# A feed-forward layer with squared ReLU: every contraction cut into 64-row halves, two matmuls at a time on the row groups of the array

## The chip, the cores and the metric

One NeuronCore of a Trainium2 chip runs the whole program. The metric is the device time of one execution in microseconds (us). "Fast" runs are those that agree with the quickest of their kernel.

The engines by their short names: PE is the matmul engine and PEld its weight loads; ACT, DVE and POOL are the scalar, vector and general-purpose engines; SP only issues transfers here. On the page of the kernel before, a product is a weight load (PEld, 128x128, 98 ns on average) and a matmul of 512 or 288 columns with those weights (PE), whose result goes to `ps`, the tensor that the kernel declares in PSUM as eight banks of 512 columns. "Contraction" is the index that a product sums over.

## The reference

```
B, S, D, F = 1, 2048, 576, 4608          # all bf16
h   = x @ w1 + b1                        # [2048, 4608], contraction over 576
r   = max(h, 0)
out = (r * r) @ w2 + b2                  # [2048, 576],  contraction over 4608
```

The number to keep in mind is 576 = 4.5 x 128. The kernel before gives the array 128 contraction rows at a time (128*128 on its page), so the first product does not fill a whole number of tiles. The second product does: 4608 = 36 x 128.

## The kernel before

x is used transposed, in four blocks of 512 rows of x (`b`). The first product makes 36 tiles of h per block (`f`), each 128 features x 512 rows, in one PSUM bank. Its contraction runs over five tiles of 128; the fifth holds the last 128 features of x, of which the first 64 were already used, and these are set to zero. ACT adds the bias and applies ReLU, DVE squares into `h2T`. The second product of a block is interleaved with the first product of the next block: five matmuls of 512 columns, then eight of 288.

```python
# first product: NJ = 5 tiles, the last one half zeros
for j in range(NJ):
    ins = pe.matmul(ps[:, bank, :], w1_sb[:, j, fs], xT_sb[:, j, bsl(b)],
                    start=(j == 0), stop=(j == NJ - 1))
...
# second product: two column halves of 288, whole 128-row tiles
for h in halves:
    ins = pe.matmul(ps[:, 4 + 2 * (q % 2) + h, 0:DH],
                    h2T[:, b % 2, f, st * P : (st + 1) * P],
                    w2_sb[:, f, h * DH : (h + 1) * DH],
                    start=(f == 0), stop=(f == NF - 1))
...
# DVE: what makes half of the fifth tile zero, and the eviction
dve.memset(xT_sb[0:DTAIL, KT, bsl(b)], 0.0)
...
dve.tensor_tensor(o_sb[...], ps[:, 4 + 2 * (q % 2) + h, 0:DH], b2_sb[...], AluOpType.add)
```

## Time and profile before

| | before |
|---|---|
| time, median of the runs of the first round | 307.97 us (307.55 to 308.4) |
| PE busy | 300.4 of 305.7 us |
| chain that ended last | 98% on PE |
| DVE, ACT busy | 114.5 us, 101.9 us |
| first matmul of the first product, last matmul of the second (starts) | 6.00 us, 302.80 us |

The page of the kernel before, first its engine sums, then its chain of waits, then its costliest groups. A group's columns are: line, engine, operation, output and inputs, shapes, count, busy time in us, mean duration of one in ns, and the engine's idle time just before them with what ended it.

```profile
PE 300.4 (98%) x1887; PEld 187.9 (61%) x1918; DVE 114.5 (37%) x184; ACT 101.9 (33%) x148; POOL 0.7 (0%) x6
...
PE 98%; issue 1%; DVE 0%; POOL 0%; POOLq 0%
...
L255 PE MATMUL ps<-xT_sb,w_sb 128*128 128x512 bf16 x689 | 167.2, 379 | 1.6
L280 PE MATMUL ps<-w_sb,h2T 128*128 128x288 bf16 x1152 | 158.8, 286 | 0.0
L339 DVE TENSOR_TENSOR h2T<-r_sb 128x512 bf16<-128x512 f32 x144 | 99.7, 692 | 152.0 <-ACT r_sb L311 151.9
L359 DVE TENSOR_TENSOR o_sb<-ps,b_sb 128x288 bf16<-128x288 f32 x32 | 13.2, 450 | 31.2 <-PE ps L280 31.2
```

PE never waits for the second product (0.0). 31 of the 720 first-product records are missing from the trace. DVE waits 151.9 us for ACT, which waits for PE. So PE bounds the kernel.

The mean durations 379 and 286 ns are not what a matmul costs, since the next one starts before the record of the last one ends (216 and 122.5 ns from start to start, as shown below). The cost is the distance between two starts, called a slot from here on. The timeline of before in an interleaved stretch (start, length, engine, line, what, count) shows it.

```profile
149.49 0.69 ACT L311 ACTIVATE r_sb<-ps,b_col 128x512 f32<-128x512 f32 x1 [1.37 <-PE ps L255]
...
150.27 1.24 PE L255 MATMUL ps<-xT_sb,w_sb 128*128 128x512 bf16 x5
151.35 1.14 PE L280 MATMUL ps<-w_sb,h2T 128*128 128x288 bf16 x8
151.55 0.69 ACT L311 ACTIVATE r_sb<-ps,b_col 128x512 f32<-128x512 f32 x1 [1.37 <-PE ps L255]
...
152.33 1.24 PE L255 MATMUL ps<-xT_sb,w_sb 128*128 128x512 bf16 x5
```

Five wide matmuls take from 150.27 to 151.35, that is 216 ns each; eight narrow ones take from 151.35 to 152.33, that is 122.5 ns each. The whole program is then 720 x 0.2157 + 1152 x 0.1225 = 155.3 + 141.1 = 296.4 us of matmul slots, which with 6.0 us ahead and 2.9 us after the last start makes the span to within 0.4 us. A gain must remove slots.

### The profile page before, as it was taken

Reading aid. Unit: us, or ns where it says so; the run is one execution under the profiler, and the core shown is the slowest. Engines: PE = TensorE matmul, PEld = TensorE weight load, DVE = VectorE, ACT = ScalarE, POOL = GpSimd, SP = SyncE. Lnnn points to the kernel's source line nnn. Section 1 sums busy time; section 2 is a strip of 40 time slices with the busy share of each in tenths; the row PEclk is TensorE's granted clock in tenths of the full one; section 3 lists DMA queues with packets and bytes.
Section 4 is the critical chain, followed back from the end, with each engine's and each line's share of the span. In section 5 each row is a group of like instructions: output and inputs, shape, how many; then the busy total and the mean of one; then the engine's idle time right before and its main releaser. Section 6 shows DMA issues by size and latency. Waiting matters only on the chain.

```text
span 305.7 us, 4424 instructions
## 1 busy us (share of the span) xinstructions
PE 300.4 (98%) x1887; PEld 187.9 (61%) x1918; DVE 114.5 (37%) x184; ACT 101.9 (33%) x148; POOL 0.7 (0%) x6
## 2 busy tenths in 40 slices
PE   8999999999999999999999999999999999999996
PEld 7444446666666666666666666666666666687874
DVE  2666663343433434334333343433333343311111
ACT  3666663233323323333332333333233333300000
POOL 0000000000000000000000000000000000000000
PEclk9999999999999999999999999999999999999999
DMA  7984996200000000000000000000000000000000
GB/s 222 354 277 91 362 349 119 57 20 0 2 19 0 21 0 20 1 0 21 0 20 2 0 21 0 19 2 0 19 2 19 2 19 0 2 19 23 19 21 19
DMA packets 22579, 16.56 MB, mean 54 GB/s; under 512 B 9376, under 2 KB 22560, under 8 KB 22560
## 3 DMA queue, kind: packets, MB, share of 16 engines
q1 hardware_dynamic: 22224, 15.98, 17.1%
q8 instruction: 15, 0.25, 0.3%
q10 hardware_dynamic: 336, 0.30, 0.3%
q14 instruction: 4, 0.03, 0.0%
HBM read 11.95 MB, written 2.36 MB: 47 GB/s over the span
## 4 chain that ended last, share of the span: by engine, by line
PE 98%; issue 1%; DVE 0%; POOL 0%; POOLq 0%
PE ps L255 50%; PE ps L280 46%; PE ps L207 1%; PE ps L217 1%; DVE o_sb L359 0%; PE ps L227 0%; PE ps L265 0%; POOL ones L197 0%; POOLq L378 0%
## 5 line engine op out<-in xcount | busy, mean ns | idle before, releaser
L255 PE MATMUL ps<-xT_sb,w_sb 128*128 128x512 bf16 x689 | 167.2, 379 | 1.6
L280 PE MATMUL ps<-w_sb,h2T 128*128 128x288 bf16 x1152 | 158.8, 286 | 0.0
L339 DVE TENSOR_TENSOR h2T<-r_sb 128x512 bf16<-128x512 f32 x144 | 99.7, 692 | 152.0 <-ACT r_sb L311 151.9
L311 ACT ACTIVATE r_sb<-ps,b_col 128x512 f32<-128x512 f32 x144 | 98.9, 687 | 161.8 <-PE ps L255 160.7
L280 PEld LDWEIGHTS ps<-w_sb,h2T 128*128 128x128 bf16 x1152 | 112.7, 98 | 48.6
L255 PEld LDWEIGHTS ps<-xT_sb,w_sb 128*128 128x128 bf16 x720 | 70.5, 98 | 64.9 <-ACT xT_sb L133 0.3
L359 DVE TENSOR_TENSOR o_sb<-ps,b_sb 128x288 bf16<-128x288 f32 x32 | 13.2, 450 | 31.2 <-PE ps L280 31.2
L207 PE MATMUL ps<-ones 128*128 128x128 bf16 x22 | 2.5, 313 | 1.1 <-POOL ones L197 1.1
L207 PEld LDWEIGHTS ps<-ones 128*128 128x128 bf16 x22 | 2.3, 147 | 1.0 <-POOL ones L197 1.0
L134 DVE CAST xT_sb<-ps 128x512 bf16<-128x512 f32 x2 | 1.3, 686 | 4.0 <-PE ps L217 4.0
L217 PE MATMUL ps<-ident,x_nat 128*128 128x128 bf16 x20 | 2.3, 309 | 0.0
L217 PEld LDWEIGHTS ps<-ident,x_nat 128*128 128x128 bf16 x20 | 2.1, 143 | 0.3 <-issue 0.3
L133 ACT ACTIVATE xT_sb<-ps 128x512 bf16<-128x512 f32 (+1 forms) x3 | 1.7, 594 | 1.4 <-PE ps L217 1.4
L133 ACT ACT_TABLE_LOAD x1 | 1.3, 1283 | 2.4 <-issue 2.4
L327 DVE MEMSET xT_sb<- 64x256 uint32 x3 | 0.8, 272 | 0.0
L323 DVE COPY b_col<-ps 128x36 f32<-128x36 f32 x1 | 0.2, 195 | 1.0 <-PE ps L265 1.0
L227 PE MATMUL ps<-ones 128*128 128x128 bf16 x3 | 0.5, 311 | 0.0
L317 DVE MEMSET b_nat<- 128x64 uint32 x1 | 0.1, 112 | 0.9 <-PEq L378 0.9
L227 PEld LDWEIGHTS ps<-ones 128*128 128x128 bf16 x3 | 0.4, 147 | 0.0
L199 POOL TENSOR_SCALAR_AFFINE_SELECT ident<-ones 128x128 bf16<-128x128 bf16 x1 | 0.3, 292 | 0.1
L318 DVE MEMSET xT_sb<- 64x256 uint32 x1 | 0.3, 272 | 0.0
L265 PE MATMUL ps<-ident,b_nat 128*128 128x128 bf16 x1 | 0.2, 219 | 0.1
(6 smaller groups left out, 0.7 us busy)
## 6 DMA issues: line engine op xcount, KB each, us to landing
w_sb<-in_w_dram SPq DMA_DIRECT2D x9, 576.0 KB, 8.2
w_sb<-in_w_dram SPq DMA_DIRECT2D x8, 512.0 KB, 6.4
out_dram<-o_sb SPq DMA_DIRECT2D x15, 144.0 KB, 1.7
w_sb<-in_w_dram SPq DMA_DIRECT2D x9, 128.0 KB, 7.3
w_sb<-in_w_dram SPq DMA_DIRECT2D x1, 384.0 KB, 3.6
x_nat<-in_x_dram ACTq DMA_DIRECT2D x2, 144.0 KB, 3.1
x_nat<-in_x_dram SPq DMA_DIRECT2D x2, 144.0 KB, 2.8
b_sb<-in_b_dram SPq DMA_DIRECT2D x1, 144.0 KB, 8.1
```

What stands on the lines that cost most here:

```text
L133: return eng.activation(dst, src, COPY)
L134: return eng.tensor_copy(dst, src)
L199: pool.affine_select(ident[:], ones[:], [[1, P]], AluOpType.is_equal, 0.0, base=0, channel_multiplier=-1).then_inc(s_id, 1)
L207: pe.matmul(ps[:, 0, 0:P], ones[:], ones[:], start=True, stop=True)
L217: ins = pe.matmul(ps[:, TB0 + j, t * P : (t + 1) * P], x_nat[:, t, d0 : d0 + P], ident[:], start=True, stop=True,)
L227: pe.matmul(ps[:, 0, 0:P], ones[:], ones[:], start=True, stop=True)
L255: ins = pe.matmul(ps[:, bank, :], w1_sb[:, j, fs], xT_sb[:, j, bsl(b)], start=(j == 0), stop=(j == NJ - 1),)
L280: ins = pe.matmul(ps[:, 4 + 2 * (q % 2) + h, 0:DH], h2T[:, b % 2, f, st * P : (st + 1) * P], w2_sb[:, f, h * DH : (h + 1) * DH], start=(f ...
L311: act.activation(r_sb[:, g % NR, :], ps[:, g % MM1_BANKS, :], RELU, bias=b1_col[:, f : f + 1]).then_inc(s_act, 1)
L327: dve.memset(xT_sb[0:DTAIL, KT, bsl(b)], 0.0).then_inc(s_xprep, 1)
L339: dve.tensor_tensor(h2T[:, b % 2, f, :], r_sb[:, g % NR, :], r_sb[:, g % NR, :], AluOpType.mult).then_inc(s_sq, 1)
L359: dve.tensor_tensor(o_sb[:, i, h * DH : (h + 1) * DH], ps[:, 4 + 2 * (q % 2) + h, 0:DH], b2_sb[:, h * DH : (h + 1) * DH], AluOpType.add,). ...
```

## The change

Half of every fifth tile multiplies zeros. The change cuts both contractions into 64-row halves. Rows 0 to 63 and rows 64 to 127 of the array (the two row groups) are then to work as two arrays of 64 rows, each with its own weights, its own moving data and its own PSUM bank. In the first product the lower rows make a tile of h from the first half of F and the upper rows one from the second half. 576 is 9 x 64, so nine slots make two tiles of h, where ten were needed before. To let both row groups go through all nine chunks, x is kept in nine tiles that hold each chunk once in the lower and once in the upper partitions; four of these are put together by DVE copies. w1 is laid out in two halves of the partitions. The second product, which has no ragged edge, is halved as well: its two halves land in two banks, and DVE adds them.

```diff
+    LO = [0, 2, 4, 6, 1, 3, 5, 7, 8]      # chunk in the lower rows, by slot
+    HI = [1, 3, 5, 7, 2, 4, 6, 8, 0]      # chunk in the upper rows
 ...
-                    for j in range(NJ):
-                        ins = pe.matmul(ps[:, bank, :], w1_sb[:, j, fs], xT_sb[:, j, bsl(b)], ...)
+                    for h in range(2):
+                        ch_ = LO[j] if h == 0 else HI[j]
+                        ins = pe.matmul(
+                            ps[:, banks[h], :],
+                            w1_sb[HP * h : HP * (h + 1), ch_, cs],
+                            xT_sb[HP * h : HP * (h + 1), j, bsl(b)], ...)
 ...
-                    for h in halves:
-                        ins = pe.matmul(ps[:, 4 + 2 * (q % 2) + h, 0:DH], h2T[:, b % 2, f, ...], w2_sb[:, f, ...], ...)
+                    for h in range(2):
+                        ins = pe.matmul(
+                            ps[:, 4 + 2 * ch + h, 0:DH],
+                            h2T[HP * h : HP * (h + 1), b % 2, f, st * P : (st + 1) * P],
+                            w2_sb[HP * h : HP * (h + 1), f, ch * DH : (ch + 1) * DH], ...)
 ...
-            dve.memset(xT_sb[0:DTAIL, KT, bsl(0)], 0.0).then_inc(s_xprep, 1)
+                dve.tensor_copy(xT_sb[0:HP, j, cs0], xT_sb[HP:P, src_lo, cs0])
+                dve.tensor_copy(xT_sb[HP:P, j, cs0], xT_sb[0:HP, src_hi, cs0]).then_inc(s_asm, 1)
 ...
-                        dve.tensor_tensor(o_sb[...], ps[:, 4 + 2 * (q % 2) + h, 0:DH], b2_sb[...], AluOpType.add)
+                    dve.tensor_tensor(t_sb[:, ch, :], ps[:, 4 + 2 * ch, 0:DH], b2_sb[:, cs], AluOpType.add)
+                    dve.tensor_tensor(o_sb[:, i, cs], ps[:, 5 + 2 * ch, 0:DH], t_sb[:, ch, :], AluOpType.add)
```

(Cut: the interleaving is by slot now, w1 is loaded in 16 transfers of 64 partitions each, and semaphores follow.)

## The prediction

> **What bounds the kernel now.** TensorE. The page's first part has PE busy 300.4 of 305.7 us, and the chain that ended last lies 98% on PE (50% first product, 46% second), with 1.6 us of idle time before all first-product matmuls and none before the second's. The granted clock is full. In the timeline ACT fires every 2.06 us in the interleaved stretches, for 5 matmuls of 512 columns and 8 of 288: 216 and 122.5 ns start to start; the durations shown (379, 286 ns) are latencies. Sum: 720 x 0.2157 + 1152 x 0.1225 = 155.3 + 141.1 = 296.4 us, plus 6.0 us before the first product and 2.5 us after the last matmul: the span. DVE (37%) and ACT (33%) wait for PE.
>
> **What the change removes.** The contraction of the first product is 576 = 4.5 x 128 and is paid as 5 tiles; half the fifth multiplies zeros. As 9 chunks of 64 rows, two on the array at a time (lower rows: one weight column block into one bank; upper rows: another into another bank), it costs 9 slots for two blocks, where it was 10: 648 slots of 512 columns for 720. Gain: 72 x 0.2157 = 15.5 us, all on the critical path. The second product is also halved in rows, 2304 half matmuls in 1152 pairs, with no column saved[...].
>
> **What it adds.**
> - Matmuls and weight loads double (1872 to 3600). A pair of second-product halves must get two weight loads into 122.5 ns. [...]
> - DVE: two additions where one 450 ns addition was (32 more: about 14 us), and 32 copies of 64x512 bf16 within SBUF [...]. DVE goes from 114 to about 137 us of 290: still half idle. Two 687 ns activations free a pair's banks, under the 1.94 us of a pair: no stall.
> - Start: nine x tiles instead of five must be ready in the first pair, four of them by DVE copies of evicted tiles; w1 comes in 64-row pieces with short rows. About +0.5 to 1 us. The end has one more addition: +0.5 us.
>
> **Predicted: 294 us** (307.97 - 15.5 + 1.5), 291 to 304 for 8 times in 10. Chances: faster by over 2% 0.80, within 2% 0.07, slower 0.13.
>
> **What would show it.** Right: starts of the two halves of a pair within tens of ns, pairs at 216 and 122.5 ns; the first product's stretch (ends at 45 us now) some 3.5 us shorter; interleaved stretches with 10% fewer 512-column slots; the closing second-product stretch (34.8 us) unchanged; PE idle under 3 us; DVE near 137 us busy.
>
> **What would make it wrong.** (1) Weight loads or issue limit the short pairs: closing stretch longer than 34.8 us, pairs above 123 ns, say 160 ns; this alone could cost 10 to 45 us and is the main risk. (2) The two row halves don't stream together: 560 us. [...] (4) The start waits for w1, or the second product for w2: gaps before the first matmuls or around 49 us, laid to DMA.

Where a cut is marked, a passage is taken out that no trace showed: why the second product is split, an estimate of two weight loads in series and the conclusion drawn from it, what was said of loads and starts on two row groups, a risk of 7 us that rested on that, and the duration put for one copy. The 1.5 us for start and end is the author's estimate. DVE's 137 us were 114.5 us and 14 us for the additions, and the rest, some 8 us, was for the 32 copies.

## The result

| | before | after |
|---|---|---|
| median | 307.77 us (16 runs, 307.28 to 308.4) | 294.14 us (8 runs, 293.58 to 294.68) |
| ratio | | 0.9554, 95% interval 0.9542 to 0.9565 |
| profiled span | 305.7 us | 292.2 us |
| DVE busy | 114.5 us | 132.9 us |

A ratio is the mean time of one kernel's fast runs over that of the other's of the same rounds, so it is not quite the ratio of the medians quoted. Run again unedited in a later session (after_again), the changed kernel gave 294.06 us (5 runs) and a ratio of 0.955 (0.9534 to 0.9565), as expected:

> The changed kernel itself, unedited, for a comparison in the same rounds with the two versions beside it: 294.1 us, ratio to before 0.955.

The page after, the same parts.

```profile
PE 286.2 (98%) x3646; PEld 181.8 (62%) x3646; DVE 132.9 (45%) x243; ACT 94.6 (32%) x150; POOL 0.7 (0%) x6
...
PE 94%; DVE 3%; DMA 1%; SPq 1%; issue 0%; ACT 0%
...
L333 PE MATMUL ps<-w_sb,h2T 64*128 64x288 bf16 x2304 | 214.6, 283 | 0.0
L306 PE MATMUL ps<-xT_sb,w_sb 64*128 64x512 bf16 x1296 | 210.9, 376 | 1.8 <-DMA w_sb<-in_w_dram 1.1
...
L429 DVE TENSOR_TENSOR h2T<-r_sb 128x512 bf16<-128x512 f32 x144 | 94.2, 689 | 113.3 <-ACT r_sb L380 113.0
...
L452 DVE TENSOR_TENSOR t_sb<-ps,b_sb 128x288 f32<-128x288 f32 x32 | 14.6, 456 | 36.6 <-PE ps L333 36.5
L457 DVE TENSOR_TENSOR o_sb<-ps,t_sb 128x288 bf16<-128x288 f32 x32 | 14.6, 457 | 1.1
L438 DVE COPY xT_sb<-xT_sb 64x512 bf16<-64x512 bf16 x24 | 6.9, 289 | 0.7
```

PE is still the bound. It issues nearly twice the matmuls, and each lasts as long as before (376 and 283 ns), yet the kernel is shorter: two run at a time. PE's busy column for a group has become useless as a cost, because pairs of the two products overlap within it (214.6 + 210.9 us is far more than the span). The timeline of the changed kernel in an interleaved stretch shows the pairs.

```profile
150.02 0.38 PE L306 MATMUL ps<-xT_sb,w_sb 64*128 64x512 bf16 x2
150.24 0.29 PE L333 MATMUL ps<-w_sb,h2T 64*128 64x288 bf16 x2
150.36 0.38 PE L306 MATMUL ps<-xT_sb,w_sb 64*128 64x512 bf16 x2
150.57 0.41 PE L333 MATMUL ps<-w_sb,h2T 64*128 64x288 bf16 x4
150.82 0.38 PE L306 MATMUL ps<-xT_sb,w_sb 64*128 64x512 bf16 x2
```

Two wide matmuls fit into 0.38 us, the length of one, and the next pair starts 0.21 to 0.22 us later. The records themselves, start in us and distance to the previous record of the same engine in ns:

```
150.019 PE          64x512        150.235 PE   +213   64x288        150.357 PE   +119   64x512
150.022 PE     +3   64x512        150.238 PE     +3   64x288        150.360 PE     +3   64x512
150.020 load                      150.236 load +212                 150.359 load +119
150.024 load   +4                 150.240 load   +4                 150.362 load   +3
```

A pair starts within 3 ns here, its two weight loads within 4 ns, and pairs follow each other at 216 and 122 ns: the slots of before. (In the first stretch, where the first product runs alone, the two starts of a pair lie 19 ns apart until 44 us; pairs still follow at 216 ns.)

Where the 13.44 us of the span went, from the starts of the first and last matmuls of the two products:

| stretch | before | after | difference |
|---|---|---|---|
| start of the program to first matmul | 6.00 | 6.82 | +0.82 |
| first to last matmul (start to start) | 296.80 | 282.01 | -14.79 |
| last matmul to the end | 2.86 | 3.39 | +0.53 |

The middle row is 72 slots x 0.2157 = 15.53 us less, and 0.74 us more of stalls. The three small losses, 2.1 us, are the difference between the gain by slots and the gain in the span. This is one profile of each kernel; in after_again the first matmul starts at 6.64 us, so the 0.82 varies by some 0.2 us.

### The profile page after: what moved, and what is told of

Its sections match the earlier page's. It is cut to its first block, busy times and chain, and to the rows that moved or that the text cites. A ratio compares the mean times of both kernels' runs of the same rounds, so it can differ in the third digit from the quotient of the medians.

```text
span 292.2 us, 8040 instructions
## 1 busy us (share of the span) xinstructions
PE 286.2 (98%) x3646; PEld 181.8 (62%) x3646; DVE 132.9 (45%) x243; ACT 94.6 (32%) x150; POOL 0.7 (0%) x6
## 4 chain that ended last, share of the span: by engine, by line
PE 94%; DVE 3%; DMA 1%; SPq 1%; issue 0%; ACT 0%
PE ps L333 48%; PE ps L306 46%; DVE h2T L429 2%; DMA w_sb<-in_w_dram 1%; DVE xT_sb L438 1%; SPq L172 0%; SPq L176 0%; ACT r_sb L380 0%; DVE t_sb L452 0%; DVE o_sb L457 0%
## 5 line engine op out<-in xcount | busy, mean ns | idle before, releaser
L333 PE MATMUL ps<-w_sb,h2T 64*128 64x288 bf16 x2304 | 214.6, 283 | 0.0
L306 PE MATMUL ps<-xT_sb,w_sb 64*128 64x512 bf16 x1296 | 210.9, 376 | 1.8 <-DMA w_sb<-in_w_dram 1.1
L333 PEld LDWEIGHTS ps<-w_sb,h2T 64*128 64x128 bf16 x2304 | 112.2, 94 | 64.3
L429 DVE TENSOR_TENSOR h2T<-r_sb 128x512 bf16<-128x512 f32 x144 | 94.2, 689 | 113.3 <-ACT r_sb L380 113.0
L380 ACT ACTIVATE r_sb<-ps,b_col 128x512 f32<-128x512 f32 x144 | 91.0, 683 | 156.7 <-PE ps L306 156.7
L306 PEld LDWEIGHTS ps<-xT_sb,w_sb 64*128 64x128 bf16 x1296 | 65.5, 94 | 41.3 <-DMA w_sb<-in_w_dram 1.2
L452 DVE TENSOR_TENSOR t_sb<-ps,b_sb 128x288 f32<-128x288 f32 x32 | 14.6, 456 | 36.6 <-PE ps L333 36.5
L457 DVE TENSOR_TENSOR o_sb<-ps,t_sb 128x288 bf16<-128x288 f32 x32 | 14.6, 457 | 1.1
L438 DVE COPY xT_sb<-xT_sb 64x512 bf16<-64x512 bf16 x24 | 6.9, 289 | 0.7
L168 ACT ACTIVATE xT_sb<-ps 128x512 bf16<-128x512 f32 x4 | 2.1, 603 | 1.2 <-PE ps L258 1.2
L401 DVE COPY xT_sb<-xT_sb 64x512 bf16<-64x512 bf16 x4 | 1.2, 290 | 0.2
L402 DVE COPY xT_sb<-xT_sb 64x512 bf16<-64x512 bf16 x4 | 1.1, 287 | 0.1
```

The lines of the kernel that those rows point to most:

```text
L168: return eng.activation(dst, src, COPY)
L306: ins = pe.matmul(ps[:, banks[h], :], w1_sb[HP * h : HP * (h + 1), ch_, cs], xT_sb[HP * h : HP * (h + 1), j, bsl(b)], start=first, stop=last,)
L333: ins = pe.matmul(ps[:, 4 + 2 * ch + h, 0:DH], h2T[HP * h : HP * (h + 1), b % 2, f, st * P : (st + 1) * P], w2_sb[HP * h : HP * (h + 1), f ...
L380: act.activation(r_sb[:, g % NR, :], ps[:, mm1_bank(b, f), :], RELU, bias=b1_col[:, f : f + 1]).then_inc(s_act, 1)
L401: dve.tensor_copy(xT_sb[0:HP, j, cs0], xT_sb[HP:P, src_lo, cs0])
L429: dve.tensor_tensor(h2T[:, b % 2, f, :], r_sb[:, g % NR, :], r_sb[:, g % NR, :], AluOpType.mult).then_inc(s_sq, 1)
```

## The experiments

Eleven edits and one repetition of the changed kernel were run. All gave correct results. Theory: the gain is the 72 wide slots that were removed, and everything else must only not spoil it. The rivals are named with each run.

### 1. The zeros put back (zero_slot)

```diff
-    SLOTS = [0, 1, 4, 2, 5, 3, 6, 7, 8]
+    SLOTS = [0, 1, 4, 2, 5, 3, 6, 7, 8, 9]      # slot 9: both row groups multiply a tile of zeros
```

> Each first-product pair gets a tenth slot that multiplies 64 rows of zeros on both row groups, so the array streams the 720 slots of before again, everything else as in the changed kernel. Theory (the gain is the 72 slots of 512 columns that were removed): 294.1 + 72 x 0.2157 = 309.7 us, about 0.5% above before (its start and end are a little longer). Rival (the packing itself makes slots cheaper or dearer than 216 ns, or the gain comes from the split second product): well off 309.7 us; near 294 if the zero slots cost little.

Measured in three rounds: 308.84 us, ratio to before 1.003 (1.0014 to 1.0047). The page of this run shows the 144 matmuls on zeros beside the 1296 others:

```profile
L314 PE MATMUL ps<-xT_sb,w_sb 64*128 64x512 bf16 x1296 | 211.6, 376 | 0.9 <-DMA w_sb<-in_w_dram 0.8
L314 PE MATMUL ps<-zx,w_sb 64*128 64x512 bf16 x144 | 27.3, 376 | 0.0
```

With the slots of before the time of before is back: +14.7 us over the changed kernel, where 15.5 were expected. The missing 0.8 us lies in the start and the stalls: in the profiled run the first matmul starts at 6.27 us (6.82 in the changed kernel's profile, a start that varies), and from the first to the last matmul 0.6 us is more than slots, where the changed kernel has 1.2. So the gain is the removed slots; packing by itself made a slot neither cheaper nor dearer (pairs at 216 and 122 ns in the changed kernel, as the whole matmuls before).

### 2. The second product left whole (mm2_whole)

```diff
-                    for h in range(2):
-                        ins = pe.matmul(ps[:, 4 + 2 * ch + h, 0:DH], h2T[HP * h : HP * (h + 1), ...], ...)
+                    ins = pe.matmul(ps[:, 4 + 2 * ch, 0:DH], h2T[:, ...], w2_sb[:, ...], ...)
```

and one addition per eviction instead of two. Everything else, the fine interleaving too, stays.

> First product in 64-row pairs, second product back to whole 128-row matmuls of 288 columns, interleaved as finely as in the changed kernel: some 970 changes between row modes. Theory [...]: each change exposes most of the latency of a matmul, 286 - 122 = about 160 ns (estimate), so 294 + 970 x 0.16 = about 450 us, PE starts after a change 160 ns later than the cadence. Rival ([...] the split was needless): 294 us or half a microsecond less, as the second addition at the end falls away.

Two passages that named a mechanism which no run shows are cut there. The 160 ns are an estimate, the length of a matmul's record less its slot.

389.05 us. The direction is the theory's, the size is not: 95 us, not 155. The timeline of this run:

```profile
150.21 0.42 PE L332 MATMUL ps<-w_sb,h2T 128*128 128x288 bf16 x2
150.56 0.39 PE L306 MATMUL ps<-xT_sb,w_sb 64*128 64x512 bf16 x2
150.88 0.42 PE L332 MATMUL ps<-w_sb,h2T 128*128 128x288 bf16 x2
151.24 0.39 PE L306 MATMUL ps<-xT_sb,w_sb 64*128 64x512 bf16 x2
151.56 0.30 PE L332 MATMUL ps<-w_sb,h2T 128*128 128x288 bf16 x1
```

A pair of the first product is now followed after 0.32 us (150.56 to 150.88) instead of 0.22. Call the use of the array as two halves or as a whole its row mode. Over the run the mean distance is 321.9 ns from a pair (its first start) to a whole matmul, where 215.7 is the slot, and 220.1 ns from a whole matmul to a pair, where 122.5 is the slot: 106 and 98 ns lost per change of row mode. A whole matmul that follows a whole one comes after 128.2 ns on average instead of 122.5. Together that is 450 x 106 + 449 x 98 + 702 x 5.7 ns, about 96 us, which is the whole loss. The trace has 899 changes (my expectation had counted 971), so by the time a change costs (389.05 - 294.14 + 0.5) / 899 = 106 ns, the 0.5 us being the addition that falls away at the end. What happens in the array at a change the trace does not show, only what it costs.

### 3. The same, with fewer changes (mm2_whole_coarse)

```diff
-                want = (len(steps) * done) // nslot
+                want = (len(steps) * done) // nslot if it[5] else 0      # only after a pair's last slot
```

> As mm2_whole, but the second product's matmuls come in one block after each first-product pair: 99 changes of row mode instead of 971. Theory (each change costs about 98 ns whatever surrounds it, from mm2_whole: (389.05 - 294.14 + 0.5) / 971): 294.1 - 0.5 + 9.7 = 303.3 us. Rival (what cost 95 us in mm2_whole was the whole matmuls or their fine mixture, not the changes): far from it, above 320 us or near 294.

304.21 us. With the 106 ns of the right count, 99 changes make 10.5 us and 304.1 us are expected; with the 98 ns 303.3. The cost is per change, not per whole matmul. (Its trace has 311 and 218 ns at the changes: 96 ns each.)

### 4. No interleaving at all (blocks)

mm2_whole again, but the order of the blocks is first product of block 0, first of 1, second of 0, first of 2, second of 1, and so on; the tile copies for blocks 2 and 3 are made while a second product runs.

```diff
-        for n in range(NPAIR):
-            for it in mm1_pair(b, n, SLOTS, True, True):
-                items.append(it)
-                ...                                        # 2.3 second-product steps after each slot
+        items += mm1_block(b) + mm2_block(b - 1)
```

> First product in 64-row pairs, second product whole, and each product of a block of 512 rows run without interleaving: 5 changes of row mode in all. Only one addition per eviction. Theory (changes cost 0.1 us each, the split second product is needed only because of the fine interleaving): 294.1 + 0.5 - 0.5 = 294 us, DVE about 19 us less busy than in the changed kernel. Rival (the interleaving hides something else, as evictions of the first product at one pair per 1.94 us): over 296 us with gaps on PE laid to ACT or DVE.

Three rounds: 294.03 us, ratio 0.9541 (0.9525 to 0.9557), the same as the changed kernel's. Five changes of mode cost the 0.5 us that the single addition at the end gives back. DVE was busy 118.3 us instead of 132.9; I had expected 19 us less and it is 14.6, the 32 additions alone (the copies stay). So the split of the second product is not part of the gain. It is the price of interleaving at the grain of single matmuls, and with PE the only bound the interleaving is not needed either.

### 5. The two halves of a pair moved apart (halves_apart)

```diff
-        return [("mm1", b, n, j, ...) for i, j in enumerate(slots)]          # lower, upper, lower, upper ...
+        return [("mm1", b, n, j, ..., h) for h in range(2) for i, j in enumerate(slots)]   # nine lower, then nine upper
```

> The same first-product half matmuls, but all nine of the lower rows first, then all nine of the upper rows, so that neighbours sit on the same row group. Theory (two halves run together only when they are neighbours in program order on different row groups): each half costs a full 216 ns slot, 294.1 + 648 x 0.2157 = about 434 us, and the first stretch of the first product alone doubles from 35 to 70 us. Rival (the queue finds independent halves further on by itself): 294 us.

338.66 us. Both theories failed: 44.5 us lost, neither 0 nor 140. The stretch of the first product alone (9 to 47 us) shows how PE orders such matmuls. The columns are the window, its length, and busy time and count of each engine.

```profile
9.00:47.00 38.00, 38.00 (x312) 18.19 (x310) 24.86 (x40) 23.38 (x34) 0.00 (x0) 1.00 0.96 218
```

312 half matmuls in 38 us are 122 ns each. If every matmul had to start after the one ahead of it in the program, only the last of nine on one row group and the first of nine on the other could overlap: eight slots of 216 ns for nine halves, 192 ns each, 198 in the window. A half takes 216 ns on its row group, so nine take 1.94 us, yet the ends of the runs of nine (the matmuls that raise the semaphore) are 1.10 us apart. A run of nine upper halves therefore begins 0.84 us before the nine lower halves ahead of it are done, that is, while three of these have not started. The starts show it: one run of nine starts its last half at 20.346 us and its row group could go on at 20.562, but the next run there begins at 20.804, just after the sixth half of the run between them (20.796), whose last three follow at 21.012, 21.228 and 21.443. So here a matmul starts ahead of three that stand before it in the program and use the other row group, and not ahead of more, though its own row group has been free for 0.24 us (20.562 to 20.804). Halves on one row group follow each other at a full slot of 216 ns (21.012, 21.228, 21.443), so halving rows without running two at a time would gain nothing. With all nine halves of a row group in one run, the gain of the pairs was lost; closer orders than this and the adjacent one were not run. (What limits the overtaking, these runs don't tell.) Most of the loss is elsewhere: the first second-product matmul starts 5.9 us later than in the changed kernel, and the interleaved stretch from there to the last first-product matmul takes 241.3 us instead of 202.3, 39.0 us more. There second-product pairs stand between the halves, too; that the same limit explains these 39 us was not tested.

### 6. How tight are the weight loads? (cols144, cols72)

The second product's halves are cut into two and then four pieces of columns, each with its own weight load. This doubles and quadruples loads and matmuls at the same number of columns.

```diff
+                    DP = DH // 2                                  # 144; // 4 for 72
-                    for h in range(2):
+                    for p_, h in [(p_, h) for p_ in range(2) for h in range(2)]:
```

Two figures in the expectations below are estimates from the trace of before. A pair's 60 ns plus about 2.5: its slots, 215.7 ns for 512 columns and 122.5 for 288, make 0.416 ns a column and 2.7 ns a matmul. The 49 ns of a load, and 98 ns for two in series: its loads last 143 to 147 ns on average in the first 6 us and 98 ns later. That this difference is what a load takes of the array is the author's guess, which no trace showed.

> The second product's half matmuls are cut into two of 144 columns each, with their own weight loads: 4608 half matmuls instead of 2304. A pair then streams for 60 ns plus about 2.5 ns. Theory (the two weight loads of a pair run side by side, as their starts 3 ns apart suggest): 62 ns per pair, 1152 x 2.5 ns more in all, about 297 us. Rival (my estimate on record: two loads in series need 98 ns): 98 ns per pair, 2304 x 98 = 226 us instead of 141 for the second product, about 379 us.

> The second product's half matmuls are cut into four of 72 columns, each with its own weight load: 9216 half matmuls. The 144-column run kept its cadence (62.5 ns a pair), so two serial loads of 49 ns are already refuted; how far does it go? Theory (the two loads of a pair run side by side and one load takes about 49 ns of the array, my estimate from the 98 and 147 ns of before): a pair can't be shorter than about 50 ns, 4608 x (50 - 32.5) = 81 us over the cadence, about 380 us. Rival (a load takes well under 30 ns of the array): 32.5 ns a pair, 4608 x 32.5 = 150 us for the second product, about 303 us.

cols144, one look: 296.87 us, as its theory had it (297). In the closing stretch of the second product alone 1064 half matmuls take 33 us:

```profile
256.00:289.00 33.00, 33.00 (x1064) 33.00 (x1059) 8.54 (x18) 0.74 (x2) 0.00 (x0) 1.00 0.07 22
```

Their starts are 62.5 ns a pair, two loads in each. That refutes the estimate that two loads need 98 ns in series.

cols72, one look: 353.38 us, and both theories failed (380 and 303). PE's timeline in the closing stretch of cols72:

```profile
302.09 2.25 PE L334 MATMUL ps<-w_sb,h2T 64*128 64x72 bf16 x128 [1.49 <-issue]
306.11 2.25 PE L334 MATMUL ps<-w_sb,h2T 64*128 64x72 bf16 x128 [1.76 <-issue]
```

Within a burst the rival was right: 128 half matmuls start within 2.06 us (the burst less the tail of its last matmul), 32.5 ns a pair. Then PE stands still, for 1.2 to 1.8 us over the whole closing stretch, always after 128 matmuls, and the profile names no engine, only "issue". 128 matmuls with their 128 loads are 256 instructions. The DMA queue named "instruction" (q8) keeps the same count: it moved 15 packets of 16 KB in the kernel before, 29 in the changed kernel and 82 in cols72, which have 3836, 7292 and 21116 matmuls and loads on PE, so 251 to 258 for each packet. The closing stretch of the changed kernel had one packet every 7 to 9 us and that of cols72 one every 3.5 to 4.6 us, one for each burst. The rate that cols72 kept up was 128 matmuls with loads per 3.78 us on average over this stretch, about 14.8 ns for each instruction. The interleaved stretch of cols72, with another mix of matmuls, runs at the same 3.77 us per 128:

```profile
55.00:279.00 224.00, 211.69 (x7599) 161.41 (x7597) 89.03 (x160) 61.67 (x98) 0.00 (x0) 1.00 0.08 17
```

cols144, with 64 pairs in 4.0 us, sits just below this rate. The changed kernel, with 64 pairs of the narrow kind in 7.8 us, is at half of it. That PE waits for the next of these packets is the author's reading of the count of 256 and of the packets' rhythm; no run shows it.

### 7. The start and the loading of w1 (start, start2, blocks_start2)

The changed kernel starts 0.82 us late and stalls some more. The first line below, of the changed kernel, ties the 1.08 us of idle time before the first matmul to w1, and the last ties 0.45 us to DVE's tile copies.

```profile
6.82 4.15 PE L306 MATMUL ps<-xT_sb,w_sb 64*128 64x512 bf16 x36 [1.08 <-DMA w_sb<-in_w_dram]
11.21 32.98 PE L306 MATMUL ps<-xT_sb,w_sb 64*128 64x512 bf16 x304 [0.24 <-issue]
44.65 5.57 PE L306 MATMUL ps<-xT_sb,w_sb 64*128 64x512 bf16 x50 [0.45 <-DVE xT_sb L438]
```

w1 lands at 217 GB/s (before: about 350), as the windows of both kernels show; the last two columns are the share of the DMA engines' time and GB/s. First before, then after.

```profile
16.00:20.00 4.00, 3.95 (x20) 1.76 (x18) 2.72 (x4) 2.51 (x4) 0.00 (x0) 1.00 1.10 349
```

```profile
20.00:23.00 3.00, 3.00 (x32) 1.58 (x28) 2.35 (x4) 1.71 (x3) 0.00 (x0) 1.00 1.12 217
```

Both windows load rows of 1 KB with the DMA engines busy throughout. Before, a transfer writes 128 partitions; after, 64.

```diff
 # start: the upper half of w1 by other queues, beside the lower half on SP
+            load_w1(act, 1, 0); load_w1(act, 1, 1)
+            for c in range(2, NWC): load_w1(pool, 1, c)
 # start2, blocks_start2: three upper pieces by ACT; the last two pieces as nine transfers over 128 partitions
+                for k in range(NCH):
+                    eng.dma_start(w1_sb[:, k, lo:hi], w1[HP * k : HP * (k + 1), :].rearrange("r (h m) -> h r m", h=2)[:, :, lo:hi])
 # all: bias column copied by ACT instead of DVE; the second block's tile copies begin two or three tiles of h earlier
```

> The changed kernel with the upper half of w1 issued from other queues (ACT's first, then POOL's) beside the lower half's, so that both halves of the partitions are written at a time, and the bias column copied by ACT instead of behind DVE's tile copies. Theory (the first product starts 0.8 us late and stalls 1.1 us in all because w1 in 64-row pieces lands late, and x of the second block behind it): first matmul at about 6.2 us instead of 6.8, no gaps after it, w1 landed by about 23 us instead of 30, 292.4 us. Rival (the landing is bound by the number of short rows, not by which partitions they go to): w1 still lands at about 30 us, 293.5 to 294 us.

> The changed kernel with another loading of w1, since the start run starved the urgent pieces behind POOL's queue and said nothing about the rate: upper halves of three early pieces go by ACT's queue beside the lower halves on SP's, the last two pieces (512 columns a half) go as nine transfers that each write all 128 partitions; bias column copied by ACT. Theory (w1 landed at 217 to 232 GB/s in the changed kernel against 350 GB/s before because each transfer writes only half of the partitions): 290 to 350 GB/s in the stretch of the last two pieces, w1 landed by about 25 us instead of 30, first matmul at about 6.2 us, the 0.8 us gap at 43.8 us gone: 292.3 us. Rival (the rate is set by the length of the rows, 1 KB here as there, or by the queue): still about 220 GB/s there, w1 at 29 to 30 us, at most 0.5 us gained.

> blocks and start2 together, meant to beat both kernels: whole second product (one addition less at the end, 0.5 us), 5 mode changes (+0.5 us), and the start and the gaps mended (1.5 to 2 us). If both causes are right and independent: about 292.2 us, ratio to before 0.949; if the loading theory fails: 294 us.

All three failed. start took 306.75 us (ratio 0.9954): three of POOL's pieces, not needed until later, landed first (7.7, 9.2 and 11.3 us), and the first piece of w1 only at 12.1 instead of 6.7 us; the bias, behind it on ACT's queue, held PE until 11.9 us. PE stood still from 5.6 to 11.9 us and from 16.0 to 20.4 us, and the granted clock was half from 8.6 to 15.4 us and from 18.8 to 25.6 us (mean 0.978). start2 took 330.43 us and blocks_start2 330.32: the eighteen transfers of 128 KB (nine for each of two pieces) were issued one every 2.7 us, and the window shows why w1 then took until 68 us.

```profile
22.00:40.00 18.00, 6.18 (x58) 2.52 (x54) 5.63 (x9) 5.06 (x8) 0.00 (x0) 0.73 0.14 49
```

Only 0.14 of the DMA engines' time was used, about two of sixteen engines, at 49 GB/s. The transfer was over 128 partitions, but its source was described as two blocks of 64 rows; that this two is what put it on two engines no run here tests. The mean granted clock of start2's profile was 0.953, so its time is not a matter of the transfers alone. These three runs thus say nothing clean about the cause of the 217 GB/s. From 8 to 23 us the changed kernel has 217 to 232 GB/s; with both queues active in start2 (4.6 to 8 us) the rate was 238 GB/s, where the changed kernel has 212 in the same window. No run here shows a transfer of w1 in this layout that writes all partitions at speed.

### 8. A version that beats both (blocks_pool)

blocks, with the bias column copied by ACT and half of the second block's tile copies made by POOL.

```diff
+            pool.wait_ge(s_x[1], 32)
+            for a, j in enumerate(ASM):
+                if a: pool.wait_ge(s_asmp, a)
+                pool.tensor_copy(xT_sb[HP:P, j, bsl(1)], xT_sb[0:HP, src_hi, bsl(1)]).then_inc(s_asmp, 1)
```

> blocks (first product in pairs, second whole, 5 mode changes), with the upper halves of the second block's four tile copies given to POOL, which is idle, and the bias column copied by ACT. Theory (the 0.8 us gap before the last slot of the second block's first pair at 43.6 us is DVE's: eight copies of 0.29 us squeezed between squares of 0.69 us; the gap at 8.7 us is the bias column behind DVE's tile copies): copies done by about 40 us, the gap gone, 0.6 us from it and 0.1 to 0.3 us from the bias column: 293.2 us, ratio to before 0.952. Rival (x lands so late that the copies can't be in time whoever makes them): the gap stays, 294 us.

Five rounds: 293.34 us (6 runs, 293.12 to 293.52), ratio 0.9519 (0.9506 to 0.9532), the best of all kernels run; the changed kernel, run again with blocks_start2's rounds, had 0.955 (0.9534 to 0.9565). The two come from different sessions, so the 0.7 us between them rests on two comparisons with before; against blocks (0.9525 to 0.9557) the intervals even overlap a little. The profiles agree with a gain: from the first to the last matmul blocks_pool takes 281.9 us, blocks 282.6, of which the gap described next is 0.6. The gap is gone: in blocks PE's timeline had a break at 44 us, in blocks_pool it runs without one from 30 to 60 us. First blocks, then blocks_pool.

```profile
44.39 0.82 PE L293 MATMUL ps<-xT_sb,w_sb 64*128 64x512 bf16 x6 [0.45 <-DVE xT_sb L424]
```

```profile
29.64 30.61 PE L303 MATMUL ps<-xT_sb,w_sb 64*128 64x512 bf16 x282
```

POOL's four copies took 3.45 us, and while they ran DVE's copies took 0.59 instead of 0.29 us and squares up to 1.04 instead of 0.69; there was time for that.

## Why the prediction was right

The prediction said 294 us (291 to 304) and the time was 294.14.

1. **What bounds the kernel, and the gain of 15.5 us.** Right. With the slots put back (zero_slot) 14.7 of it went away again.
2. **The pairs run at the old slots, 216 and 122.5 ns.** Right, with starts 3 ns apart (19 ns in the first stretch). This was the bet of the prediction, with 0.13 for slower, and it was not shown: the trace of before has no pairs.
3. **"A pair of second-product halves must get two weight loads into 122.5 ns."** It did. That the room would be tight was argued from the estimate of 98 ns for two loads in series: it took the loads of the first 6 us, 143 to 147 ns on average, for loads at half clock, and the trace shows no lower clock there (1.00 in the windows from 1 to 6 us). The two loads of a pair start 3 to 4 ns apart, and pairs with their loads follow each other at 32.5 ns within the bursts of cols72, so the room was there nearly fourfold; the nearest limit seen is another one, the 14.8 ns for each instruction over the whole closing stretch of cols72. The summed durations of the loads do not measure this room: they are 189.9 us in a span of 305.7 before (62%) and 344.5 in 292.2 after (118%), while PE has no idle time before the second product (0.0) in either.
4. **Why the second product is split as well.** The reason given, that a change of row mode costs time, was shown by no trace then. It was right in kind: in mm2_whole a change cost 106 ns, and 899 of them 95 us. But its expectation had 160 ns, and blocks shows that the split can be avoided altogether by changing mode five times.
5. **Start +0.5 to 1 us, end +0.5 us.** Measured +0.82 and +0.53. Not in the sum were 0.74 us of stalls in between. "PE idle under 3 us" held (1.8 us before the first product, 1.1 of them before its first matmul). The 1.6 us of idle time that the prediction read in the kernel before were missing records.
6. **DVE near 137 us.** Measured 132.9: additions +14.6 us as expected for the second ones, copies 9.2 us where some 8 were put (0.289 us each), and the squares' sum of busy time fell by 5.5 us, which the prediction had left alone (one still lasts 689 ns; they now come in twos that overlap: two take 1.29 us).
7. **First stretch 3.5 us shorter.** The second block's first matmul starts at 42.29 us, in the kernel before at 45.25 us: 3.0 us. The closing stretch was to stay as it was, and did: the last 290 pairs start 122.5 ns apart, as the last 296 matmuls of before do.

That the sum came out within 0.2 us is partly luck, since two small errors offset each other: the losses were 2.1 us where 1.5 were put, and the base of 307.97 us was 0.2 us above the later median.

## What to carry to other kernels

When a contraction is not a multiple of 128, the slots spent on padding are a loss on a PE-bound kernel (here 72 slots, 15.5 us), and 64-row halves of two output tiles won them back here at full rate (pairs at 216 and 122.5 ns) with the two halves of a pair adjacent in the program; with nine of one row group before nine of the other the kernel took 338.66 us. Count the changes between row modes (0.1 us each here) and either put everything into one mode or group the work by mode. Before cutting matmuls smaller, count instructions: in cols72 PE got through 256 of them per 3.8 us and no more.
